# Attention scores of four heads on own 32 rows, masked in PSUM, with one exp per group

## The chip, the cores and the metric

The kernel runs on one core of a Trainium2 chip. The time is the device time of one execution in microseconds; the number given is the median of several runs. The profile is one traced execution; its span, from the first to the last instruction, is a little shorter than the time of a run.

Names of the engines in the profile: PE is TensorE (matrix products), PEld its weight loads, DVE is VectorE, ACT is ScalarE, POOL is GpSimd and SP is SyncE, which here only issues transfers.

## The reference, cut to what matters

Two independent parts stand side by side in the output.

Part A is a long convolution: a 4-tap shift of `k`, times `v`, convolved over 2048 positions with `ssm_k` for each of 640 channels (an FFT in the reference), plus a skip term, times `q`.

Part B is attention with 32 heads of 20 dimensions, in four segments of 512 tokens that are attended causally, and a memory of the earlier segments:

```python
for s in range(N):                                   # N = 4, L = 512, Dh = 20
    logits = einsum('bhqd,bhkd->bhqk', qs, ks) * scale + mask    # mask: -1e9 above the diagonal
    p = softmax(logits)
    a_dot = einsum('bhqk,bhkd->bhqd', p, vs)
    pq = phi(qs)                                     # phi(t) = t + 1 or exp(t)
    a_mem = (pq @ M) / (pq @ z + 1e-6)
    o = g * a_mem + (1 - g) * a_dot
    M, z = M + phi(ks).T @ vs, z + sum(phi(ks))
return o @ wo
```

The change touches the line of the logits, its mask and the exp in the softmax, and how all the work is ordered.

## The kernel before, in words

Everything is recorded first and emitted in another order. `Recorder` stands in for the engines: each call becomes an `Op` with its dependences, and all products into one PSUM bank until another engine reads it form one `Op`. `plan` (line 236) then lists the work: it prices each operation by a small model (`price`), walks forward and backward with priorities from the tables `BIAS` and `HOLD`, keeps the best of seven orders, and gives banks to operations. `emit` (line 430) issues the calls in that order, so nearly every row of the profile carries the line number 435. Each engine executes its own instructions in the order emitted.

Part A is cut into five slices of 128 channels. For each slice: the shift as 16 products of 128 columns per bank (`kshift`, tiles `kr`, `skd`), a forward transform of two signals (`fwd`, `Wf` with `vt` and `kT`), butterflies and a pointwise product on VectorE (tiles `F`, `Xh`, `Kh`, `pr`, `S`), and an inverse transform (`inverse`, `Wi` with `S`). `kT` is reordered by a copy on VectorE before it is transposed.

Part B is cut into eight units `u` of one segment and half of the heads (16). For each unit: `proj` (line 688) makes K, Q and V for four blocks of 128 tokens; ScalarE copies K and Q to `KQ`, with each head's 20 values in a slot of 32, and two transposing transfers write `KT` and `QT`, where one head occupies 32 partitions and four heads fill 128. `bound` (line 710) computes for each query an upper bound of its logits, negated, and writes it by four small transfers into row 20 of each head in `QT`; row 20 of K holds ones, so the product subtracts the bound and the exp cannot overflow. I call it the bound row. Four groups `g` of four heads follow.

In `attn` (line 764) a score product contracts all 128 partitions, so one head's keys have to stand alone: `spread` (line 757) copies K from `KT` into `KZ`, where each head has its own zero-filled copy with only its 21 rows set. For a pair of heads and each of three specifications of key blocks (block 0: 512 columns; blocks 1 and 3 together: 384 + 128; block 2: 256), a product fills a bank `st` and an exp on ScalarE writes it to `ET`, transposed scores with keys on partitions. Then VectorE multiplies the diagonal blocks of `ET` by the triangle `cmask`, in two instructions per group of heads, and products of 21 columns (`o<-Va,ET`) sum over the keys; one more product per 128 queries reads the memory (`Mbd`, `PqT`). VectorE divides and writes `o_s`, which is transposed to `oT` and multiplied by `wo` once both halves of a segment are there.

PSUM has eight banks of 512 fp32 columns. They are dealt to four kinds of work: three for scores, two for part A, two for projections and one for `o`.

```python
BANKS = {"st": 3, "a": 2, "b": 2, "o": 1}      # line 836
```

Of the kernel before, what the change touches and what calls it, by code (L numbers as in the profile page):

```python
# [42 lines left out]
def small_consts():  # L43
    p = np.arange(128)
    d = p % 32
    hl = p // 32
    sel = np.zeros((128, 4, 16), np.float32)
    for g in range(4):
        ok = d < DH
        sel[p[ok], g, 4 * hl[ok] + g] = -1.0  # L50
    maskbd = np.zeros((128, 4, VW), np.float32)
    epsrow = np.zeros((128, 4), np.float32)
    for hh in range(4):
        rows = (hl == hh) & (d < DH)
        maskbd[rows, hh, 0:DH + 1] = 1.0
        epsrow[32 * hh + DH + 1, hh] = EPS
    kk = np.arange(128)[:, None]; qq = np.arange(128)[None, :]
    cmask = (kk <= qq).astype(np.float32)
    return sel.astype(BF16_NP), maskbd.astype(BF16_NP), epsrow, cmask.astype(BF16_NP)
# [21 lines left out]
class Op:  # L81
    __slots__ = ("eng", "calls", "key", "bank", "new", "dur", "lat", "dma", "pred", "succ", "tail", "idx", "late")


class Bank:
    def __init__(self, kind, home):
        self.kind, self.home, self.left, self.last, self.ops, self.seq = kind, home, 0, None, [], 0
# [6 lines left out]
class Recorder:  # L94


    def __init__(self, tc):
        self.tc, self.real = tc, tc.nc
        self.nc = ProxyNC(self)
        self.ops, self.key = [], ("const",)  # L100
        self.live, self.masks = {}, {}
        self.slots, self.home, self.turn, self.rows = {}, {}, {}, {}
# [5 lines left out]
    def bank(self, kind):  # L108
# [3 lines left out]
        b = self.home[t[:].tensor.name] = Bank(kind, t[:].tensor.name)  # L112
        b.row = kind if kind in ("st", "o") else self.key[0] if kind == "b" and self.key[0] == "P" else None
        if b.row:
            b.seq = self.rows.get(b.row, 0)
            self.rows[b.row] = b.seq + 1
# [18 lines left out]
    def add(self, eng, method, args, kw):  # L135
# [12 lines left out]
        if op is None:  # L148
            op = Op()
            op.eng, op.calls, op.key, op.bank, op.dma, op.idx = e, [], self.key, bank, None, len(self.ops)  # L150
            op.new = bank is not None and bank.last is None
            op.pred, op.succ, op.dur, op.lat = {}, [], 0.0, 0.0
            self.ops.append(op)
            if bank is not None:
                bank.left += 1
                bank.ops.append(op)
# [3 lines left out]
        self.price(op, method, outs[0], ins)  # L160
# [18 lines left out]
    def price(self, op, method, out, ins):  # L179
        n = int(np.prod(list(out.shape)[1:]))  # L180
        two = lambda a: mybir.dt.size(a.dtype) == 2
        if method == "matmul":
            op.dur += max(n / 2.4 + 2.5, 27.0)
            op.lat = 260.0
        elif method in ("dma_start", "dma_start_transpose"):
            src = ins[0]
            size = int(np.prod(list(out.shape))) * mybir.dt.size(out.dtype)
            if method == "dma_start_transpose":
                packets, per = size / 256, 23.5
                dram = src.space == bass.MemoryType.DRAM  # L190
                op.dur = 650.0 + 560.0 * size / 131072 + (600.0 if dram else 0.0)
            else:
                run = min(self.run(out), self.run(src))
                packets, per = size / run, max(23.0, 13 + 0.042 * run)
                op.dur = 640.0 if op.eng != "ACT" else 650.0
            op.dma = packets * per / 16
            op.lat = 1200.0
        elif op.eng == "ACT":
            op.dur, op.lat = n / 1.152 + 33, 210.0
        elif op.eng == "DVE":  # L200
            fast = all(two(a) and a.space != bass.MemoryType.PSUM and int(a.ap[-1][0]) == 1 for a in [out] + ins)
            if method == "tensor_tensor":
                op.dur = n / (1.92 if fast else 0.96) + 60
            elif method == "tensor_reduce":
                op.dur = int(np.prod(list(ins[0].shape)[1:])) / 0.96 + 60
            elif method == "reciprocal":
                op.dur = 67 + 6.1 * n
            else:
                op.dur = n / (3.84 if fast else 1.2) + 60
            op.lat = 150.0  # L210
        else:
            op.dur, op.lat = 100 + n / 1.2, 200.0

    @staticmethod
    def run(ap):
        r = mybir.dt.size(ap.dtype)
        need = 1
        pat = list(ap.ap)[1:] if ap.space != bass.MemoryType.DRAM else list(ap.ap)
        for st, n in reversed(pat):
            if st != need:  # L220
                break
            r *= n
            need *= n
        return r

    def finish(self):
        for o in self.ops:
            o.dur, o.lat = int(round(o.dur)), int(round(o.lat))
            o.dma = None if o.dma is None else int(round(o.dma))
            if o.new and o.bank.kind == "a":  # L230
                for q in o.bank.ops[1:]:
                    for p in q.pred.values():
                        if p.bank is not o.bank:
                            o.pred[p.idx] = p

    def plan(self, bias, hold, passes, slack):

        ops = self.ops
        for o in ops:
            o.succ = []  # L240
        for o in ops:
            for p in o.pred.values():
                p.succ.append(o)
        for o in ops:
            o.late = list(o.pred.values())
        for o in ops:
            if o.new:
                for b in o.bank.ops[1:]:
                    for q in o.succ:
                        if q.bank is not o.bank and b not in q.late:  # L250
                            q.late.append(b)
        for o in reversed(ops):
            o.tail = max([q.tail for q in o.succ], default=0) + o.dur + (o.dma or 0) + o.lat
        load = [o.dma is not None and o.dma > 0 and o.key[0] in ("load", "A", "P", "const") and len(o.pred) <= 1 for o in ops]
        best = None
        prio = [-(o.tail + bias.get(o.key, 0)) for o in ops]
        held = [hold.get(o.key, 0) if o.dma is not None else 0 for o in ops]
        for n in range(passes + 1):
            total = self.forward(prio, held)
            if best is None or total < best[0]:  # L260
                best = (total, self.order, self.slot, self.start, self.done)
            if n == passes:
                break
            back, end = self.backward([-(self.start[o.idx] + o.dur) for o in ops])
            lead = [end - b for b in back]
            prio = [s - (bias.get(o.key, 0) >> 3) for o, s in zip(ops, lead)]
            held = [max(0, s - slack - hold.get(o.key, 0)) if l else 0 for o, s, l in zip(ops, lead, load)]
        _, self.order, self.slot, self.start, self.done = best
        return best[0]

    @staticmethod
    def lag(o):
        return o.lat if o.dma is None else max(1150 - o.dur, -50) + o.dma + 450

    def backward(self, prio):
        ops = self.ops
        need = [0] * len(ops)
        for o in ops:
            for p in o.late:
                need[p.idx] += 1  # L280
        ready = [0] * len(ops)
        free = {e: 0 for e in ("PE", "DVE", "ACT", "POOL", "SP")}
        pending, avail = {e: [] for e in free}, {e: [] for e in free}
        empty = {k: [0] * len(v) for k, v in self.slots.items()}
        row = {k: n - 1 for k, n in self.rows.items()}
        left, held = {}, set()
        times = [0]
        for o in ops:
            if need[o.idx] == 0:
                ready[o.idx] = self.lag(o)  # L290
                heapq.heappush(pending[o.eng], (ready[o.idx], o.idx))
                times.append(ready[o.idx])
        heapq.heapify(times)
        back, count = [0] * len(ops), 0
        while times:
            t = heapq.heappop(times)
            while times and times[0] <= t:
                heapq.heappop(times)
            for e in free:
                pe, av = pending[e], avail[e]  # L300
                while pe and pe[0][0] <= t:
                    i = heapq.heappop(pe)[1]
                    heapq.heappush(av, (prio[i], -i))
                if free[e] > t:
                    continue
                put_back, o = [], None
                while av:
                    x = heapq.heappop(av)
# [654 lines left out]
```

## Time and profile before

| what | value |
|---|---|
| time, median of 3 runs | 358.62 us (356.18 to 363.19) |
| profiled span | 353.7 us |
| busy share of PE, DVE, ACT, POOL | 86%, 86%, 79%, 23% |
| mean granted clock of TensorE | 0.970 |
| chain that ended last | PE 33%, DVE 28%, issue 14%, DMA 8%, ACT 6% |
| exps of scores (`ET<-st`) | 384 instructions, 185.2 us busy |
| score products (`st<-QT,KZ`) | 508 recorded, 105.1 us busy |
| masks (`ET<-ET,cmask`) | 64 instructions, 43.0 us busy |
| spreads (`KZ<-KT`) | 64 issues on GpSimd, 40.0 us busy |

Three engines are busy for four fifths of the span or more, and the chain of waits passes from one to another all the time, so no single row is the bound. Busy time is the union of the instructions' durations. On TensorE and ScalarE instructions overlap, so the mean duration of a row times its count is more than its busy time, and both are more than the time that the engine needs for it. The page's 40 slices show a head of about five slices with little ScalarE work, a long full stretch, and a short tail. It helps to ask for busy time by stretch and to read single rates off the timeline, where an unbroken run of equal instructions gives the time of one.

### The profile page before, as it was taken

The numbers are of one execution on the slowest core, as the hardware profiler recorded it, in microseconds if no ns is written. First come the engines' busy times: TensorE is split into PE (matmuls) and PEld (weight loads), VectorE is DVE, ScalarE is ACT, GpSimd is POOL, SyncE is SP. The second block draws the span as 40 slices with busy tenths as digits, with TensorE's granted clock in tenths as the row PEclk, the third lists the DMA queues.
The fourth block names the chain that finished last, engine by engine and source line by source line (L and its number), as shares of the span: only waits on it lengthen the run. The fifth ranks groups of instructions, "written<-read, shape, count | busy, mean of one in ns | idle before, by whom it ended". The sixth has DMA issues, their size and how long they took to land.

```text
span 353.7 us, 9016 instructions
## 1 busy us (share of the span) xinstructions
PE 302.4 (86%) x3462; PEld 217.8 (62%) x3466; DVE 305.7 (86%) x539; ACT 278.0 (79%) x633; POOL 80.5 (23%) x127
## 2 busy tenths in 40 slices
PE   0179699899997699799999999999989998888584
PEld 0157477567785477577766776777766675555363
DVE  2016999999999999899999999999998998999960
ACT  1046648999979989889989999989986998899502
POOL 9402410214112110312024005230060040312023
PEclk9999999999999899899999999999998999999869
DMA  9976766969557335705598358537430564302043
GB/s 262 212 141 165 159 141 98 256 117 199 112 114 186 73 62 113 134 17 74 150 130 202 74 126 142 117 68 105 100 92 26 91 105 70 92 30 69 0 101 110
DMA packets 110267, 40.97 MB, mean 116 GB/s; under 512 B 102624, under 2 KB 107264, under 8 KB 109968
## 3 DMA queue, kind: packets, MB, share of 16 engines
q1 hardware_dynamic: 100768, 29.50, 43.7%
q0 software_dynamic: 5088, 8.09, 8.9%
q10 hardware_dynamic: 4368, 2.81, 2.8%
q8 instruction: 27, 0.44, 0.5%
q14 instruction: 16, 0.13, 0.1%
HBM read 13.36 MB, written 5.24 MB: 53 GB/s over the span
## 4 chain that ended last, share of the span: by engine, by line
PE 33%; DVE 28%; issue 14%; DMA 8%; ACT 6%; SPq 6%; POOL 3%; POOLq 0%; ACTq 0%; DVEq 0%
PE b L435 13%; PE a L435 9%; PE st L435 7%; DVE S L435 7%; SPq L435 6%; PE o L435 4%; DVE ET L435 4%; DMA KT<-KQ 3%; DVE Xh L435 3%; ACT ET L435 3%; DVE kam L435 3%; DMA kr<-in_A_k_dram 2%; POOL out_dram L435 2%; DMA oT<-o_s 1%; DVE o L435 1%
## 5 line engine op out<-in xcount | busy, mean ns | idle before, releaser
L435 ACT ACTIVATE ET<-st 128x512 bf16<-128x512 f32 (+1 forms) x384 | 185.2, 575 | 11.6 <-PE st L435 10.5
L435 PE MATMUL st<-QT,KZ 128*128 128x384 bf16 (+2 forms) x508 | 105.1, 301 | 6.3 <-ACT ET L435 3.9
L435 PE MATMUL b<-wqkv,xT 128*128 128x320 bf16 x480 | 79.3, 303 | 18.8 <-DMA xT<-in_B_x_dram 16.0
L435 PEld LDWEIGHTS <-xT 128*128 128x128 bf16 x480 | 45.8, 99 | 37.6 <-DMA xT<-in_B_x_dram 16.0
L435 POOL DMA_DIRECT2D KZ<-KT x64 | 40.0, 629 | 123.0 <-PE st L435 91.1
L435 PEld LDWEIGHTS <-KZ 128*128 128x128 bf16 x512 | 45.6, 98 | 28.0 <-issue 12.2
L435 PEld LDWEIGHTS <-ET 128*128 128x128 bf16 x1280 | 41.8, 96 | 24.1 <-DVE ET L435 11.5
L435 PE MATMUL o<-Va,ET 128*128 128x21 bf16 x1280 | 44.2, 173 | 12.0 <-DVE ET L435 5.9
L435 ACT CAST F<-a 128x512 bf16<-128x512 f32 x80 | 48.4, 624 | 5.5 <-PE a L435 5.0
L435 ACT CAST KQ<-b 128x320 bf16<-128x320 f32 x64 | 30.0, 472 | 19.4 <-PE b L435 17.4
L435 DVE TENSOR_TENSOR ET<-ET,cmask 128x1024 bf16<-128x1024 bf16 x64 | 43.0, 682 | 0.4 <-ACT ET L435 0.4
L435 PEld LDWEIGHTS <-Wf 128*128 128x128 bf16 x320 | 30.3, 99 | 15.8 <-issue 8.8
L435 DVE TENSOR_TENSOR S<-S 128x2048 bf16<-128x2048 bf16 (+1 forms) x40 | 37.2, 950 | 0.2
L435 POOL DMA_DIRECT2D out_dram<-outa x20 | 15.4, 769 | 71.5 <-DVE outa L435 52.7
L435 PE MATMUL b<-wo,oT 128*128 128x320 bf16 x160 | 28.0, 314 | 0.6 <-DMA oT<-o_s 0.6
L435 PE MATMUL a<-kT,Wf 128*128 128x256 bf16 x160 | 24.3, 274 | 2.9 <-DVE outa L435 1.9
L435 ACT CAST outb<-b 128x320 bf16<-128x320 f32 x32 | 14.9, 480 | 14.1 <-PE b L435 14.1
L435 DVE TENSOR_TENSOR o<-o,rr 128x320 bf16<-128x320 f32 x48 | 23.6, 491 | 1.6
L435 PE MATMUL a<-vt,Wf 128*128 128x256 bf16 x160 | 23.3, 280 | 1.4 <-ACT F L435 0.7
L435 PE MATMUL a<-S,Wi 128*128 128x256 bf16 x160 | 22.2, 286 | 1.5 <-DVE S L435 1.5
L435 DVE TENSOR_TENSOR S<-Xh,Kh 128x4096 bf16<-128x4096 bf16 x10 | 22.8, 2284 | 0.1
L435 PE MATMUL a<-skd,kr 128*128 128x128 bf16 x320 | 22.0, 224 | 0.4 <-DMA kr<-in_A_k_dram 0.2
(61 smaller groups left out, 385.0 us busy)
## 6 DMA issues: line engine op xcount, KB each, us to landing
KZ<-KT POOLq DMA_DIRECT2D x64, 42.0 KB, 2.9
kT<-in_A_ssm_k_dram SPq DMA_DIRECT2D x5, 512.0 KB
qd<-in_A_q_dram SPq DMA_DIRECT2D x20, 128.0 KB
out_dram<-outa POOLq DMA_DIRECT2D x20, 128.0 KB, 2.8
out_dram<-outb POOLq DMA_DIRECT2D x16, 160.0 KB, 2.1
vt<-in_A_v_dram SPq DMA_DIRECT2D x16, 128.0 KB
Wf<-c_wf ACTq DMA_DIRECT2D x1, 1024.0 KB
Wi<-c_wi SPq DMA_DIRECT2D x1, 1024.0 KB
```

The source lines that it names most:

```text
L435: f(*[fix(a) for a in args], **{k: fix(v) for k, v in kw.items()})
```

## The change

The change has four parts.

1. **Scores on own rows.** K and Q of a unit go into one tile `KQT`, by one transposing transfer instead of two. The score product of head `hl` reads only that head's rows, `32*hl` to `32*hl + 20`, of K and of Q. `KZ` and its spreads are gone. The four heads of a group stand on four separate sets of 32 rows of the array and write four separate banks.
2. **One exp.** The four banks are one tile `st` of 2048 columns, and one exp reads all four heads: three exps per group of heads (2048, 2048 and 1024 columns) instead of twelve.
3. **Masks in PSUM.** Before the scores a product of the identity with `later` (0 on and below the diagonal, -1e9 for keys later than the query) is written to each diagonal block, and the score product adds to it. VectorE's masks are gone.
4. **One pool and a stored order.** The other four banks are one pool `w` for all other work. There is no planner: the order of the operations is stored as a compressed list, and each group takes the bank that has been free longest. Some operations change place: the `kT` copies go from VectorE to ScalarE; most plain loads and the bound rows go from the queues of SP and ACT to GpSimd's; `Wf` is loaded in four pieces.

The purpose is to relieve VectorE of the masks, ScalarE of the fixed cost of many small exps, GpSimd and the transfer engines of the spreads, and to let four products with a short contraction share the array.

```diff
-        QT, PqT, Va = self.QT[half], self.PqT[half], self.Va[half]
+        KQT, PqT, Va = self.KQT[half], self.PqT[half], self.Va[half]
+        QT = KQT[:, 4:8, :]
...
-        def spread(gg):
-            def f():
-                for hl in range(4):
-                    rows = slice(32 * hl, 32 * hl + DH + 1)
-                    nc.gpsimd.dma_start(out=self.KZ[gg][rows, :, hl, :], in_=self.KTs[u][rows, 2 * gg:2 * gg + 2, :])
-            return f
...
-                for hp in range(2):
-                    for spec in (((0, 0),), ((1, 0), (3, 384)), ((2, 0),)):
-                        sts = [self.bank("st") for j in range(2)]
-                        width = 0
-                        for j in range(2):
-                            hl = 2 * hp + j
-                            for (kc, c0) in spec:
-                                n = L - 128 * kc
-                                nc.tensor.matmul(sts[j][:, c0:c0 + n], lhsT=KZ[:, g % 2, hl, 128 * kc:128 * kc + 128], rhs=QT[:, g, 128 * kc:L], start=True, stop=True)
...
-                        for j in range(2):
-                            nc.scalar.activation(out=ET[:, 2 * hp + j, e0:e0 + width], in_=sts[j][:, 0:width], func=ACTF.Exp, scale=SCALE)
-                for (c0, step) in ((0, 512), (896, 128)):
-                    blk = ...
-                    V.tensor_tensor(out=blk, in0=blk, in1=self.cmask[:, None, None, :].to_broadcast([128, 4, 2, 128]), op=ALU.mult)
+                for spec in (((0, 0),), ((1, 0), (3, 384)), ((2, 0),)):
+                    st = self.bank("st")[:].rearrange("p (h q) -> p h q", h=4)
+                    nd = len(spec)
+                    for hl in range(4):
+                        blk = st[:, hl, 0:128] if nd == 1 else st[:, hl, :].rearrange("p (b q) -> p b q", q=128)[:, 0:4:3, :]
+                        later = self.later[:] if nd == 1 else self.later[:, None, :].to_broadcast([128, 2, 128])
+                        nc.tensor.matmul(blk, lhsT=self.ident[:], rhs=later, start=True, stop=False, skip_group_check=True)
+                    for (kc, c0) in spec:
+                        n = L - 128 * kc
+                        for hl in range(4):
+                            rows = slice(32 * hl, 32 * hl + DH + 1)
+                            nc.tensor.matmul(st[:, hl, c0:c0 + n], lhsT=KQT[rows, g, 128 * kc:128 * kc + 128], rhs=KQT[rows, 4 + g, 128 * kc:L],
+                                             start=False, stop=True, skip_group_check=True)
+                    width = max(c0 + L - 128 * kc for (kc, c0) in spec)
+                    e0 = ET_OFF[spec[0][0]]
+                    nc.scalar.activation(out=ET[:, :, e0:e0 + width], in_=st[:, :, 0:width], func=ACTF.Exp, scale=SCALE)
...
-                nc.sync.dma_start_transpose(out=self.KTs[u][:, :, tok], in_=KQ[:, 0, :, :])
-                nc.sync.dma_start_transpose(out=QT[:, :, tok], in_=KQ[:, 1, :, :])
+                nc.sync.dma_start_transpose(out=KQT[:, :, tok], in_=KQ[:])
...
-                nc.sync.dma_start(out=QT[r:r + 1, :, :], in_=bT[4 * hl:4 * hl + 4, :])
+                nc.gpsimd.dma_start(out=KQT[r:r + 1, 4:8, :], in_=bT[4 * hl:4 * hl + 4, :])
...
-            nc.vector.tensor_copy(out=skp[:], in_=sk.rearrange("d (b p c) -> d c b p", b=4, c=4))
+            nc.scalar.copy(out=skp[:], in_=sk.rearrange("d (b p c) -> d c b p", b=4, c=4))
...
-BANKS = {"st": 3, "a": 2, "b": 2, "o": 1}
+BANKS = {"st": (1, 2048), "w": (4, 512)}
...
-    rec.finish()
-    rec.plan(BIAS, HOLD, PASSES, SLACK)
+    order = np.frombuffer(zlib.decompress(base64.b85decode(ORDER)), np.uint16).tolist() if ORDER else range(len(rec.ops))
     with tc.manual_schedule():
-        rec.emit()
+        rec.emit(order)
```

## The prediction

> **What bounds the kernel now.** I read the page's first two parts, then busy time by stage, then the groups by shape, then the timeline where single costs can be read off. The page alone does not name a bound:
>
> ```profile
> PE 302.4 (86%) x3462; PEld 217.8 (62%) x3466; DVE 305.7 (86%) x539; ACT 278.0 (79%) x633; POOL 80.5 (23%) x127
> ```
>
> The stretches do. I cut the span at the first and last exp of scores (53.4 and 333 us; columns as in the header):
>
> ```profile
> core 0: us, PE busy (x) PEld busy (x) DVE busy (x) ACT busy (x) POOL busy (x), PEclk, DMA share, GB/s
> 0.00:53.40 53.40, 31.57 (x292) 22.99 (x293) 27.22 (x46) 20.64 (x44) 19.47 (x30) 1.00 0.80 179
> 53.40:333.00 279.60, 257.16 (x3057) 185.26 (x3058) 269.48 (x478) 254.00 (x582) 55.86 (x89) 0.98 0.53 106
> 333.00:354.00 21.00, 13.71 (x116) 9.57 (x116) 9.05 (x17) 3.41 (x8) 5.21 (x8) 0.74 0.35 89
> ```
>
> In the 279.6 us of the score stage VectorE is busy 269.5 us, 96%. That stage is VectorE-bound, and TensorE (92%) and ScalarE (91%) are close behind; the other 74 us are a head that waits for loads and a tail. Two groups of the score stage, all from the table by shape:
>
> ```profile
> L435 ACT ACTIVATE ET<-st 128x512 bf16<-128x512 f32 x256 | 146.0, 647 | 9.9 <-PE st L435 9.3
> L435 ACT ACTIVATE ET<-st 128x256 bf16<-128x256 f32 x128 | 48.8, 431 | 1.7 <-PE st L435 1.2
> L435 DVE TENSOR_TENSOR ET<-ET,cmask 128x1024 bf16<-128x1024 bf16 x64 | 43.0, 682 | 0.4 <-ACT ET L435 0.4
> L435 DVE COPY kT<-kT 128x2048 bf16<-128x2048 bf16 x5 | 7.3, 1467 | 4.2 <-DMA kT<-in_A_ssm_k_dram 4.2
> ```
>
> Busy time of PE and ACT includes overlapped latency, so I take rates from unbroken runs in the timeline:
>
> ```profile
> 26.68 0.23 PE L435 MATMUL a<-Drow,cmask 1*128 1x128 bf16 x1
> 26.84 0.39 PE L435 MATMUL a<-kT,Wf 128*128 128x256 bf16 x2
> 27.16 0.22 PE L435 MATMUL a<-Drow,cmask 1*128 1x128 bf16 x1
> 27.32 2.61 PE L435 MATMUL a<-kT,Wf 128*128 128x256 bf16 x16
> 30.05 1.95 PE L435 MATMUL a<-skd,kr 128*128 128x128 bf16 x32
> ...
> 61.14 2.08 ACT L435 ACTIVATE ET<-st 128x512 bf16<-128x512 f32 x4
> 63.06 0.64 ACT L435 CAST F<-a 128x512 bf16<-128x512 f32 x1
> ```
>
> 32 products of 128 columns take 1.95 us, less a 0.22 us latency of the last: 0.056 us each. In the same way 256 columns take 0.109, 320 columns 0.136, 384 about 0.162, 512 0.216 and the 21-column products 0.026 us. Four exps of 512 columns take 1.92 us to the next instruction: 0.478 each, that is 0.833 ns per column and 0.05 us. One alone lasts 0.61 us (0.38 for 256), so its end, which a waiting TensorE sees, comes after 0.833 ns per column and 0.18 us. In the waits between the two engines ACT starts 0.04 us after the product's end, and PE 0.05 us after the exp's end.
>
> **What the Trainium skill says.** "TensorE: Matmul & The Clock Gate", Part 3 (Packing small matmuls): products on different groups of 32 rows run concurrently in the array; four with K=32 and N=512 measured 3.07 times faster. No product of the kernel before is packed, so the trace cannot confirm it. "TensorEngine Tiling (Array Packing)", Key Properties: changing the tiling mode drains TensorE. The trace agrees and prices it: the one-row Drow product uses a 32-row tile; two 256-column products before it would stream in 0.22 us, but it starts 0.32 us after them, and the next full product starts 0.16 us after it instead of 0.056. Each switch costs 0.10 us. The same page, PSUM Pressure: different row tiles must write different banks, which is why the four heads get four banks. "ScalarE: Activation LUTs", What ACT_TABLE_LOAD costs: 0.833 ns per element, a fixed part of 186 ns for an instruction with immediate operands, and about 93 ns overlap of neighbours. The trace has 0.833, 180, and 130 ns overlap.
>
> **The change part by part.**
>
> *VectorE.* The 64 masks (43.0 us) go, and the five kT copies (7.3 us) move to ACT. In the score stage that is 41.6 + 3.9 us, so VectorE falls from 269.5 to 224 us there. It stops being the bound.
>
> *ScalarE.* Of 384 exps 96 remain: 64 of 2048 columns, 32 of 1024. Throughput before 256 x 0.478 + 128 x 0.265 = 156 us; after 64 x 1.76 + 32 x 0.90 = 141 us. The five copies add 5 x 1.8 = 9 us (the 2048-column PqT row lasts 1.91). Net about -6 us: ScalarE hardly gets lighter. Its other work between the first and last exp sums to 90 us by the order, 230 us in all.
>
> *TensorE.* Score products streamed 128 x (0.216 + 0.162 + 0.109 + 0.056) = 69.5 us. After, per score group of four heads: identity products 4 x 0.056 = 0.22 us (0.44 for the group with two diagonals), one mode switch in (0.10), then the packed scores. Three 0.026 us issue steps and the stream make 0.216 + 0.08 = 0.29 us for 512 columns (the skill's 3.07 would give 0.28), 0.34 for 384 + 128, 0.19 for 256. So 0.62, 0.88 and 0.51 us, 2.0 us per four heads, 64 us in total, plus 96 switches back, 9.6 us. TensorE's stream is thus the same as before, about 74 for 70 us: packing pays for the masks. Unpacked, the scores would take 0.86, 0.87 and 0.44 us and the total becomes 107 + 9.6 us.
>
> *The new wait.* One four-bank score buffer instead of three: group n+1's identity products wait on TensorE's in-order queue until exp n has ended, and everything behind them waits too. Conversely exp n+1 waits on ACT's queue for the group, with evacuations behind it. Round trip seen by TensorE: exp end (1.89 or 1.03 us), plus 0.25 us for both hand-overs and the product's latency: 2.13 and 1.28 us. The stored order puts other products in this gap. Summing the products between neighbouring score groups of the new PE order with the rates above, switch back included: 2.20 us on average behind a long exp, 1.39 behind a short one. Each gap costs the larger of filling and round trip: 2.33 x 64 + 1.46 x 31 = 194.3 us. Add the score groups, 63.3 us: 257.6 us. In 26 gaps ACT's own evacuations are longer than that, +6 us: 263.5 us for the stage if nothing else interrupts.
>
> *Losses on top.* A clock of 0.98 in this stage, as before, is 2% of 247 us of TensorE stream: 5 us. Before, the stage lost 10 us over its bound; with four banks for all other groups instead of five, and two engines now locked together, I take 7 us (0 to 25). Stage: 275 us.
>
> *Head and tail.* Before the first score group stand 228 products, 24.0 us of stream, instead of 288; the bound row goes through GpSimd's queue, KZ's spread (64 transfers) no longer stands between KT and the scores, and K and Q come in one transpose. Loads still hold the first product (16.0 us in the trace). I take the first exp at 46 us (43 to 52) instead of 53.4. At the end the last mask stood behind other VectorE work (exp over at 332.7, product at 339.5), which now vanishes; the transposes, output projection and store remain: 17 us (15 to 21) instead of 21.
>
> *Hidden anyway.* Transfers moved from SP to GpSimd: its queue sheds 64 spreads (40.0 us at 0.63 each) and takes 77 issues (32 bound rows, 20 loads of q, 16 of v, 4 of ssm_k, five of weights), some 48 us of a 23% busy engine. Behind a load that waits for its buffer stand, in order, bound rows and stores; the scores of a later unit wait for the rows, which the order issues a unit ahead, so I charge nothing beyond the losses above. Wf in four pieces: inside the head.
>
> Sum: 46 + 275 + 17 = 338 us of span. The median was 4.9 us above the profiled span (358.6 against 353.7), so the time is 343 us.
>
> **The rivals.** (a) *The packed products do not overlap*, or overlap little. For it: no trace here shows packing, and identity products at full height alternate with them. Against: the skill's measurement, and separate banks. The same sum gives 302 us; with 12 us of losses, 46 + 314 + 17 + 4.9 = 382 us, slower. (b) *The single buffer locks PE and ACT together*: each late transfer, VectorE result or missing bank now delays both, with no spare score bank to absorb it. For it: ACT is above 90% and three banks absorbed such jitter. Against: the order's fillings match the round trip. With 27 us of losses the stage takes 290 to 295, the time 355 to 361, no change. (c) *Losses nearly vanish*, since VectorE at 224 us releases banks early: stage 264, head 43, tail 16, time 328.
>
> **How the numbers follow.** Forecast 0.60, (c) 0.12, (b) 0.16, (a) 0.12. The prediction is the likeliest case, 343 us. The range runs from (c)'s value, 328, to past (b), 366: it leaves out (a) and a fast corner, under 2 in 10. Below 351.4 us are the forecast and (c): 0.72; within 2% (b): 0.15; above: 0.13.
>
> **What would show it.** VectorE about 255 us busy with no mask row; exp rows near 1.89 and 1.03 us; packed 512-column score products starting about 0.03 us apart rather than 0.22, which decides (a); score stage near 275 us, with the waits "PE st from ACT ET" and "ACT ET from PE st" short and frequent; first exp near 46 us. I am wrong if the four products of a group stand one after the other, if waits on w banks or on ACT exceed some 30 us on PE, or if the bound row's path through GpSimd delays the first scores.

## The result, and the profile after

| what | before | after |
|---|---|---|
| time, median of 5 runs each | 362.04 us (356.18 to 365.87) | 337.92 us (334.0 to 343.83) |
| ratio, 95% interval | | 0.940 (0.929 to 0.951) |
| ratio when measured again (`after_again`) | | 0.933 (0.926 to 0.940) |

The change takes 6 to 7% off, 22 to 24 us. The first profiled execution of the changed kernel was a longer one than its median, so the lines below are from the second, of 336.64 us; likewise the profile of the old order without masks, of an execution of 1581.65 us, isn't read, and that of the added VectorE load is of an execution 3 us over the mean of those in its ratio.

The page, its first lines and the chain that ended last:

```profile
span 334.8 us, 9219 instructions
...
PE 291.8 (87%) x3850; PEld 208.6 (62%) x3850; DVE 263.3 (79%) x470; ACT 268.0 (80%) x350; POOL 82.1 (25%) x139
...
PE 47%; DVE 14%; DMA 13%; ACT 12%; issue 8%; POOL 2%; SPq 2%; ACTq 0%; POOLq 0%; DVEq 0%
```

VectorE lost 42 us of busy time and its share of the chain fell from 28% to 14%; TensorE's share rose from 33% to 47%. Now the three stretches, cut at the first and the last exp as before (columns: us; busy us of PE, PEld, DVE, ACT, POOL; clock; DMA share; GB/s):

```profile
0.00:48.80 48.80, 28.70 (x241) 19.99 (x242) 17.20 (x38) 21.63 (x43) 11.37 (x28) 0.97 0.83 172
48.80:320.80 272.00, 255.17 (x3528) 182.83 (x3529) 243.09 (x427) 243.14 (x299) 66.92 (x105) 0.96 0.54 104
320.80:335.00 14.20, 7.97 (x85) 5.78 (x82) 3.05 (x8) 3.21 (x8) 3.84 (x7) 0.97 0.47 118
```

The head lost 4.6 us, the score stage 7.6 (279.6 to 272.0), the tail 6.8: 19 us of the 22 to 24, since the profile of the kernel before is of an execution shorter than its median. This split compares two single executions. The head varies most: in three traces of the old order the first exp comes at 53.0, 53.4 and 59.4 us, in six of the new one, those without the memset of the last experiment, at 48.4 to 51.3. The score stage also took in work that the kernel before did outside it: VectorE's busy time in the head fell from 27 to 17 us. In the stage VectorE is now 89% busy instead of 96%, ScalarE 89%, TensorE 94%.

The groups by shape, and two lines of the waits (us, times, longest):

```profile
L191 ACT ACTIVATE ET<-st 128x2048 bf16<-128x2048 f32 x64 | 121.5, 1898 | 11.0 <-PE st L191 9.9
...
L191 ACT ACTIVATE ET<-st 128x1024 bf16<-128x1024 f32 x32 | 33.5, 1047 | 7.9 <-PE st L191 7.8
...
L191 PE MATMUL st<-later,ident 128*128 128x128 bf16 x256 | 25.4, 223 | 3.3 <-ACT ET L191 2.8
...
L191 PE MATMUL st<-KQT 21*128 21x512 bf16 x128 | 12.7, 388 | 0.0
```

```profile
ACT ET L191 <- PE st L191: 17.7, 26, 2.4
...
PE st L191 <- ACT ET L191: 7.6, 11, 1.7
```

The same two waits in the kernel before:

```profile
ACT ET L435 <- PE st L435: 10.5, 22, 1.7
...
PE st L435 <- ACT ET L435: 3.9, 12, 0.7
```

One group of four heads on TensorE's timeline (start, us), with the products behind it:

```profile
77.80 0.39 PE L191 MATMUL st<-later,ident 128*128 128x128 bf16 x4
78.12 0.39 PE L191 MATMUL st<-KQT 21*128 21x512 bf16 x4
78.45 0.85 PE L191 MATMUL w<-wqkv,xT 128*128 128x320 bf16 x5
```

96 exps of 1.90 and 1.05 us stand where 384 stood, and no row of masks is left on VectorE. The row `st<-KQT` of 512 columns shows the packing at once: 128 products, each 0.388 us long, were busy for 12.7 us together, so four run side by side. On the timeline, four of them take the array for 0.33 us (78.12 to 78.45). With the single score buffer, ScalarE waited in 26 of the 96 hand-overs and TensorE in 11, 25 us in all; with three banks it was 14 us. What a second buffer would save was not tried.

### The profile page after: what moved, and what is told of

Its sections match the earlier page's. It is cut to its first block, busy times and chain, and to the rows that moved or that the text cites. A ratio compares the mean times of both kernels' runs of the same rounds, so it can differ in the third digit from the quotient of the medians.

```text
span 342.1 us, 9219 instructions
## 1 busy us (share of the span) xinstructions
PE 292.9 (86%) x3850; PEld 209.6 (61%) x3850; DVE 263.1 (77%) x470; ACT 268.6 (79%) x350; POOL 82.3 (24%) x139
## 4 chain that ended last, share of the span: by engine, by line
PE 43%; DVE 21%; DMA 14%; ACT 9%; issue 9%; POOL 2%; SPq 0%; POOLq 0%; DVEq 0%; ACTq 0%
PE w L191 34%; PE st L191 9%; DMA KQT<-KQ 8%; DVE S L191 6%; ACT ET L191 5%; DMA xT<-in_B_x_dram 4%; DVE Kh L191 2%; DVE pr L191 2%; ACT F L191 2%; DVE kam L191 2%; DMA vt<-in_A_v_dram 2%; DVE o L191 1%; POOL out_dram L191 1%; DVE outa L191 1%; DVE Xh L191 1%
## 5 line engine op out<-in xcount | busy, mean ns | idle before, releaser
L191 ACT ACTIVATE ET<-st 128x2048 bf16<-128x2048 f32 (+1 forms) x96 | 154.7, 1612 | 20.5 <-PE st L191 19.4
L191 PE MATMUL w<-wqkv,xT 128*128 128x320 bf16 x480 | 79.5, 311 | 18.6 <-DMA xT<-in_B_x_dram 16.4
L191 PEld LDWEIGHTS <-xT 128*128 128x128 bf16 x480 | 45.4, 101 | 42.4 <-DMA xT<-in_B_x_dram 16.4
L191 PE MATMUL st<-later,ident 128*128 128x128 bf16 (+1 forms) x384 | 45.5, 242 | 8.3 <-ACT ET L191 7.9
L191 ACT CAST F<-w 128x512 bf16<-128x512 f32 x80 | 44.8, 606 | 1.4 <-PE w L191 1.3
L191 PEld LDWEIGHTS <-ident 128*128 128x128 bf16 x384 | 31.8, 100 | 19.0 <-issue 13.7
L191 PE MATMUL w<-Va,ET 128*128 128x21 bf16 x1280 | 43.4, 173 | 0.0
L191 ACT CAST KQ<-w 128x320 bf16<-128x320 f32 x64 | 26.5, 449 | 13.6 <-DMA KQT<-KQ 8.9
L191 PE MATMUL st<-KQT 21*128 21x512 bf16 (+3 forms) x512 | 35.6, 309 | 0.4 <-DMA KQT<-bT 0.4
L191 PE MATMUL w<-wo,oT 128*128 128x320 bf16 x160 | 25.6, 299 | 2.4 <-DVE o L191 1.3
L191 PE MATMUL w<-vt,Wf 128*128 128x256 bf16 x160 | 23.6, 277 | 1.3 <-DVE xm L191 0.6
```

What stands on the lines that cost most here:

```text
L191: f(*[fix(a) for a in args], **{k: fix(v) for k, v in kw.items()})
```

## The experiments

Every ratio is to the kernel before on the same chip, with its 95% interval. All runs of the changed kernel are to be held against 0.933. They undo one part and keep the stored order, which stands for all parts together; with an order of its own each of them might lose less.

### The changed kernel again

> The changed kernel itself, for a second profile. Its first profile has first exp at 49.5 us, 279.3 us from first to last exp (279.6 in the kernel before), and a tail of 14 us, with one stop of TensorE and ScalarE of 7 us near 96-103 us, when KQT transposes wait among 16 other loads. Theory 1 (VectorE was the bound of the score stage and its relief pays): an ordinary run has a stage of 268-274 us, first exp 46-49, span 332-337, ratio about 0.94; the stop near 100 us is shorter or gone. Theory 3 (the stage is not shorter, only head and tail are): stage within 3 us of 279.6, span 340.

Ratio 0.933 (0.926 to 0.940), profile as above: the stage is 272.0 us, 7.6 us shorter where theory 3 allowed 3, so theory 3 falls by this one execution, though head and tail together (11.4 us) gave more than the stage. The stop near 96 us is short here: ScalarE waited 2.39 us for a KQT transpose at 86 us.

### Masks back on VectorE

```diff
-                        nc.tensor.matmul(blk, lhsT=self.ident[:], rhs=later, start=True, ...)
+                for (c0, step) in ((0, 512), (896, 128)):
+                    blk = ET[...]
+                    V.tensor_tensor(out=blk, in0=blk, in1=self.later[...], op=ALU.mult)
```

Here `later` holds ones and zeros, and the score products start their banks themselves.

> In the changed kernel the masks go back to VectorE: the identity products are left out and the two multiplications of ET per group of heads stand where the exp that they need ends; everything else, with its order, stays. VectorE gets 64 x 0.68 = 43 us back, TensorE loses 32 x 0.88 = 28 us. Theory 1: VectorE is the bound again, 244 + 42 = 286 us busy in the stage, which with 2-4% idle gives 292-298 us, ratio 0.99-1.01 (355-362 us). Theory 2 (packing is what pays, VectorE had slack left): TensorE is lighter, so no slower than the changed kernel, ratio 0.90-0.95.

Ratio 1.084 (1.072 to 1.096): 54 us more than the changed kernel, beyond every expectation. Its stage, and its waits:

```profile
48.40:375.70 327.30, 251.93 (x3146) 166.31 (x3147) 279.57 (x488) 245.68 (x299) 66.29 (x104) 0.88 0.41 85
```

```profile
DVE ET L192 <- ACT ET L192: 37.3, 31, 3.7
...
PE w L192 <- DVE o L192: 27.0, 18, 3.0
...
ACT ET L192 <- PE st L192: 26.2, 20, 3.3
```

VectorE is only 280 of 327 us busy, so its load alone doesn't set this stage. A mask must wait for its exp; VectorE's queue stood 37.3 us in 31 such waits, TensorE waited for the results queued behind (27.0 us), and ScalarE for TensorE's scores (26.2 us). The masks stand right behind their exps, where the stored order had no place for them. The clock of this stage is lower too, 0.88 instead of 0.96, and no run separates it from the waits.

### The load of the masks without their wait

```diff
+                    if spec[0][0] > 0:
+                        blk = self.load[...]          # a tile that nothing else uses
+                        V.tensor_tensor(out=blk, in0=blk, in1=self.later[...], op=ALU.mult)
```

> The changed kernel with 64 more VectorE instructions of the masks' form (128x1024, 0.68 us each) on a tile that nothing else uses: 43 us of load, 42 in the score stage, no wait for an exp and nobody waiting for them; the identity products stay. If the VectorE load as such was the price: 243 + 42 = 285 us busy in the stage, which takes 288-298 us, ratio 0.98-1.01. If it was the wait between exp, mask and product that cost the 55 us with masks on VectorE: 0-8 us more, ratio 0.935-0.955.

Ratio 0.987 (0.983 to 0.991), 19 us above 0.933, or above 0.934 for the kernel that shares this one's memset (the hold below). The stage:

```profile
44.30:343.80 299.50, 259.67 (x3527) 184.31 (x3526) 278.26 (x491) 245.35 (x299) 67.58 (x105) 0.95 0.51 94
```

VectorE is again over 90% busy (278 of 299.5), and the load as such has a price, as the first of the two expectations says. So about 19 of the 54 us come with the load alone. The other 35 come with the waits and with the lower clock of the run before (0.88; here 0.95).

### No masks at all in the changed kernel

```diff
-                        nc.tensor.matmul(blk, lhsT=self.ident[:], rhs=later, start=True, stop=False, ...)
```

> The changed kernel without any mask: the identity products are left out and nothing takes their place, so the attention is not causal. TensorE loses 28 us of stream. If TensorE together with the hand-over to ScalarE paces the stage (my sum): 15-28 us shorter, ratio 0.86-0.90. If VectorE (244 us busy in 279) or ScalarE (about 235 us of throughput) still paces it: 0-8 us shorter, ratio 0.92-0.94.

Ratio 0.937 (0.931 to 0.943): no gain. The stage takes 270.6 instead of 272.0 us, with TensorE 232.6 busy instead of 255.2:

```profile
51.30:321.90 270.60, 232.62 (x3146) 160.77 (x3147) 242.34 (x426) 241.46 (x299) 66.50 (x104) 0.94 0.55 103
```

The chain that ended last:

```profile
PE 22%; DVE 21%; DMA 20%; ACT 20%; issue 10%; POOL 3%; SPq 1%; POOLq 0%; DVEq 0%; ACTq 0%
```

So the masks cost the changed kernel nothing: TensorE takes them in time that it would otherwise wait. TensorE alone isn't its bound, although it has 47% of the chain: without the masks its share falls to 22%, those of VectorE, ScalarE and the transfers rise, and the time stays. This contradicts the sum of the prediction, by which the stage had to become 15 to 28 us shorter.

### Full-height score products

```diff
-    lhsT=KQT[rows, g, 128 * kc:128 * kc + 128], rhs=KQT[rows, 4 + g, 128 * kc:L]
+    lhsT=KQT[:, g, 128 * kc:128 * kc + 128], rhs=KQT[:, 4 + g, 128 * kc:L]
```

> The score products of the changed kernel read all 128 rows of K and Q instead of 32 each, so each computes the sum over four heads and four of them can't stand side by side; no change of tiling mode any more. Per four heads TensorE streams 4 x (0.216 + 0.162 + 0.056 + 0.109) = 2.17 us of scores instead of 0.85, and saves 0.6 us of mode changes: +0.7 us, +23 us in all, and the round trip grows as long. Theory 2 (packing pays, TensorE is near its limit): +18 to +30 us, ratio 0.99-1.03. Theory 1 alone (TensorE has slack once VectorE is relieved): +0 to +8 us, ratio 0.94-0.965.

Ratio 0.989 (0.980 to 0.998): 20 us more, within theory 2's 18 to 30. The stage and the chain:

```profile
49.50:338.20 288.70, 276.53 (x3500) 215.79 (x3527) 243.90 (x424) 246.04 (x299) 66.92 (x105) 1.00 0.49 97
```

```profile
PE 71%; ACT 10%; DMA 8%; issue 6%; POOL 2%; SPq 1%; DVE 1%; POOLq 0%; ACTq 0%; DVEq 0%
```

TensorE is 96% busy and 71% of the chain. Packing is needed: without it, nearly all that the change gains is gone. Together with the last run: TensorE has no gain left in it, and no room either.

### Four exps instead of one

```diff
-    nc.scalar.activation(out=ET[:, :, e0:e0 + width], in_=st[:, :, 0:width], func=ACTF.Exp, scale=SCALE)
+    for hl in range(4):
+        nc.scalar.activation(out=ET[:, hl, e0:e0 + width], in_=st[:, hl, 0:width], func=ACTF.Exp, scale=SCALE)
```

> The changed kernel with the one exp over four banks cut into four over one bank each, placed one after the other. Each costs ScalarE 0.05 us more: 288 x 0.05 = 14.7 us, and the hand-over back to TensorE comes 0.15 us later. If ScalarE together with the hand-over paces the stage: 10-20 us more, ratio 0.96-0.99. If ScalarE has slack: 0-5 us more, ratio 0.935-0.95.

Ratio 0.955 (0.947 to 0.963), from two executions: 8 us more, just under the first band and over the second. About half of 14.7 us of ScalarE time comes through.

### The kernel before without masks, planned anew

```diff
-                for (c0, step) in ((0, 512), (896, 128)):
-                    blk = ...
-                    V.tensor_tensor(out=blk, in0=blk, in1=self.cmask[...], op=ALU.mult)
```

> The kernel before without its two masks per group of heads: the attention is not causal, and the planner orders the rest anew. Theory 1 (VectorE, 269 of 280 us busy, bounds the score stage): VectorE falls to about 228 us there and the stage to what ScalarE and TensorE allow, 12-25 us less, ratio 0.93-0.965. Theory 3 (the score stage is not what the change shortens): 0-5 us less, from the tail alone, ratio 0.985-1.0.

Ratio 1.004 (1.000 to 1.007). By the numbers expected theory 1 falls. But the first exp now comes at 61.3 us instead of 53.4:

```profile
0.00:61.30 61.30, 35.39 (x308) 25.81 (x309) 33.10 (x49) 20.45 (x43) 19.37 (x30) 0.97 0.71 166
61.30:340.90 279.60, 256.78 (x3082) 188.46 (x3089) 238.62 (x423) 253.14 (x583) 58.56 (x93) 0.98 0.53 105
```

The planner chose another order, with more work ahead of the first score (308 products instead of 292; TensorE's wait for xT is the same, 16.1 us and 16.0), and VectorE is only 85% busy in a stage as long as before. Two things changed at once, so the next three kernels kept the order.

### The kernel before in its own order: no masks, shorter exps, both

The plan is made with the masks; the edits are at the issue. The first leaves out the masks, the second shortens the exps:

```diff
             for eng, method, args, kw in o.calls:
+                if eng == "vector" and "in1" in kw and is_ap(kw["in1"]) and kw["in1"].tensor.name == self.mask:
+                    continue
...
+                if eng == "scalar" and kw.get("out") is not None and kw["out"].tensor.name in self.ets:
+                    n = int(kw["out"].ap[-1][1])
+                    cut = n * 456 // 512
+                    kw = dict(kw, out=kw["out"][:, 0:cut], in_=kw["in_"][:, 0:cut])
```

With the shorter exps, VectorE also sets the two buffers of `ET` to zero at the start, 2.19 us each.

> The kernel before in exactly its own order, planned with the masks, but the 64 mask instructions are not issued (attention not causal): 43 us of VectorE work gone, nothing else moved on any engine. Theory 1 (VectorE bounds the score stage): 15-25 us less there and up to 5 in the tail, ratio 0.92-0.955. Theory 4 (three engines in balance, in fixed orders that wait on each other, so that relief of one alone buys little): 2-8 us less, ratio 0.975-0.995. If the new order was what spoiled the run without masks and with a new plan (no gain), this run gains; if not, it is at 1.0 again.

> The kernel before in its own order, but each exp covers 456 of 512 or 228 of 256 columns, the rest of ET is zero from the start: 256 x 0.0467 + 128 x 0.0233 = 14.9 us of ScalarE throughput gone, as much as the one exp over four banks saves. Theory 1: ScalarE isn't the bound, 0-4 us less, ratio 0.99-1.0. Theory 4: 2-8 us less, 0.975-0.995. If ScalarE is the bound: 11-15 us less, 0.957-0.97.

> Both of these: no mask instructions and the shorter exps, in the order of the kernel before. Theory 1: as without masks alone, or 3-5 us less than that (0.91-0.95), since ScalarE becomes the next bound. Theory 4: clearly more than the sum of the two single gains, 18-28 us less, 0.92-0.95, while each alone stays at 0.975 or above.

| in the order of before | ratio | us |
|---|---|---|
| no masks | 0.970 (0.964 to 0.976) | -11 |
| shorter exps | 0.996 (0.992 to 1.000) | -2 |
| both | 0.950 (0.941 to 0.960) | -18 |

The stages with shorter exps alone, then with both:

```profile
59.40:338.60 279.20, 256.34 (x3057) 184.62 (x3058) 269.03 (x478) 242.96 (x582) 56.32 (x89) 0.98 0.54 106
```

```profile
53.00:318.60 265.60, 251.42 (x3070) 184.72 (x3073) 235.74 (x415) 240.52 (x582) 56.03 (x89) 0.99 0.56 111
318.60:337.80 19.20, 12.22 (x102) 8.70 (x101) 7.83 (x15) 3.42 (x8) 5.23 (x8) 0.79 0.42 97
```

With ScalarE 11 us lighter and VectorE still 96% busy, the stage stays at 279 us. It starts at 59.4 us because in this execution TensorE waited for xT until 21.9 us instead of 16.0; that moves it, but not its length. With VectorE lighter as well the stage falls to 265.6. So of these two engines VectorE was the first bound, as theory 1 has it, but of 43 us taken from it only 11 come through: less than theory 1's 15 to 25 and more than theory 4's 2 to 8. Relief of TensorE alone was not tried in this order. Once the masks are gone, ScalarE's relief is worth 7 us where it was worth 2. The sum of the single gains is 3.5%, both together 5.0%, from two executions; the difference is barely outside the intervals.

### The kernel before with scores on own rows

```diff
-    lhsT=KZ[:, g % 2, hl, 128 * kc:128 * kc + 128], rhs=QT[:, g, 128 * kc:L]
+    lhsT=KT[rows, g, 128 * kc:128 * kc + 128], rhs=QT[rows, g, 128 * kc:L]
```

> The kernel before with its score products on the 32 rows of each head: no KZ, no spreads, two buffers of KT, four of outb, everything else as it was (two banks for two heads, four exps of 512 per two heads, masks on VectorE); the planner orders anew, and two neighbouring products of different heads can stand side by side. TensorE is relieved by up to half of 70 us of score stream, less some 0.1 us per change of tiling mode (up to 2 x 192, so 10-38 us net gain at most). Theory 1 (VectorE bounds the stage): 0-6 us less, ratio 0.98-1.0. Theory 2 (TensorE's stream bounds it): 12-25 us less, ratio 0.93-0.965.

Ratio 1.050 (1.043 to 1.057), slower, which neither theory expected. The stage:

```profile
61.60:355.80 294.20, 280.47 (x3024) 161.90 (x3023) 264.49 (x468) 253.68 (x576) 20.85 (x33) 0.90 0.43 89
```

TensorE is busy for 280 us instead of 257, but its clock is 0.90 instead of 0.98, and 257 x 0.98 / 0.90 is 280: the clock alone would account for the longer busy time, and no relief by packing shows. By the starts in the trace, only 116 of 512 score products begin within 10 ns of the score product ahead of them, and the order goes over from other products to scores 166 times; in the changed kernel it is 383 of 512 and 96. It looks as if own rows pay only where the order puts the heads next to each other in different banks, but this is not shown. The run doesn't decide between the theories, because the order is new as well and the clock lower, and what lowers the clock stays open.

### Loads held back at the start

```diff
+        nc.gpsimd.memset(self.load[:], 0.0)      # 4.4 us, ahead of GpSimd's loads
```

> The changed kernel with one GpSimd memset of 4.4 us on an unused tile ahead of its queue of loads, nothing else. In the run with the added VectorE load, which had this memset too, xT landed 10.8 us after its issue instead of 14.9, since the three weight loads of 400 KB from GpSimd's queue started 4.3 us later, and the first exp came at 44.3 us instead of 48.8. If the head's gain stays: 3-5 us less than the changed kernel, ratio 0.918-0.926. If something later waits for the delayed weights or takes it back: ratio 0.93-0.94.

Ratio 0.934 (0.928 to 0.940): no gain. The chain of the changed kernel, then of this one, near its start and near 80 us:

```profile
2.01 14.93 DMA xT<-in_B_x_dram
...
78.61 7.71 DMA KQT<-KQ
```

```profile
2.02 11.07 DMA xT<-in_B_x_dram
...
43.03 1.88 ACT ET L192
...
81.88 14.27 DMA KQT<-KQ
96.14 0.02 issue
96.16 0.02 ACTq L192
96.18 0.04 issue
96.22 0.43 ACT KQ L192
96.66 0.04 issue
96.70 1.87 PE w L192 x8
```

The head's gain is there: xT lands 3.9 us sooner, and the first exp comes at 43.0 instead of 48.8 us. In this execution it is given back 50 us later. A KQT transpose takes 14.27 us instead of 7.71; the copy to KQ waits for it, TensorE waits for the copy, and both stand for over 7 us. Busy time and DMA share by tens of microseconds (changed kernel ahead):

```profile
80.00:90.00 10.00, 7.58 (x98) 5.02 (x97) 8.64 (x14) 7.61 (x12) 3.66 (x5) 0.91 1.17 238
90.00:100.00 10.00, 10.00 (x117) 6.83 (x115) 8.84 (x16) 9.17 (x17) 0.00 (x0) 0.91 0.75 137
```

```profile
80.00:90.00 10.00, 9.45 (x115) 6.38 (x114) 9.73 (x17) 8.67 (x14) 2.83 (x4) 1.00 1.11 162
90.00:100.00 10.00, 3.30 (x24) 1.87 (x24) 5.11 (x9) 3.30 (x6) 0.00 (x0) 0.70 0.66 65
```

The DMA engines are full just then (share 1.1), with the loads of `Wi` (1 MB), `wo` (800 KB), `qd`, `vt` and `kT` that the change put on GpSimd's queue. That these loads delay the transposes is read from this overlap; moving them was not tried. Nor does the overlap explain the length: in the changed kernel the share is 1.2 in the same stretch and the transpose takes 7.71 us, and in the changed kernel's longer execution, of 343.83 us, one takes 14.3 us without any hold. So the hold is not what makes a transpose slow; only that the time gained nothing is shown.

## Why the prediction was right

343 us was forecast, 337.9 measured, inside the range. The direction holds, and so does the main step, that packing pays for the masks. That the sum comes so close is in part luck: the head was 2.8 us longer than forecast, the stage 3.0 and the tail 2.8 shorter, and the stage came out although one engine's load in it and the term that was to pace it were wrong. Point by point:

- **VectorE bounds the score stage; the masks' removal ends that.** Right against ScalarE: in the order of before, relieving ScalarE alone left the stage at 279 us, relieving VectorE saved 11 us of the whole time. The size of its relief was off. I subtracted whole rows (50.3 us), but rows of VectorE overlap too, and the union fell by 42.4; and 10 us of its head work moved into the stage. It is 243 us busy there, not 224, so it still stands beside ScalarE (243) and TensorE (255).
- **Packing pays for the masks.** Right, and without this step most of the gain does not come: unpacked, 20 of 24 us are lost. The size was too cautious. I took issue steps of 0.026 us, held up by the 3.07 times of "TensorE: Matmul & The Clock Gate"; the starts in the trace lie 3 to 4 ns apart. The same page of the Trainium skill has that too, about 4 ns per further product (Measured speedup vs the span model), and the trace agrees: it was the figure to take. The time from the first identity product to the first product after the scores is 0.65, 0.86 and 0.54 us for the three groups (medians), 2.05 us per four heads, where I had 2.31 with the switch back: 66 instead of 74 us. The switch itself was right: 0.15 us from the last identity product to the first score (0.056 + 0.10), and 0.317 us from the last of four 512-column scores to the next full product (0.216 + 0.10).
- **One exp.** 1.90 and 1.05 us where I had 1.89 and 1.03. Cutting it into four costs 8 of the 14.7 us of ScalarE time.
- **The single score buffer.** I summed the larger of filling and round trip over all gaps, 263.5 us, and added 12 of losses, 275. The stage took 272. But this sum is not what sets the stage: by it the run without identity products had to be 15 to 28 us shorter there, and it was 1.4 us shorter. VectorE and ScalarE are each busy for 243 us of it, so either may hold it where TensorE does not, and a clock of 0.94 instead of 0.96 may have taken some of what that run spared TensorE. The lock of rival (b) did not come: the waits between the two engines rose from 14 to 25 us together.
- **Head.** 46 us forecast, 48.8 measured. I left the first product at 16.0 us; here it waited for xT until 17.0 us, which is 1 us of the 2.8, and the rest isn't traced. In the six traces of the new order without the hold it waited until 16.0 to 17.1 us, in the two with the memset until 12.8 and 13.1: the weight loads that moved to GpSimd's queue do delay xT. The hold also shows that ending this gains nothing in the whole time.
- **Transfers to GpSimd, charged at nothing.** Wrong in that place: I named what is queued behind a waiting load on GpSimd, but not that its big loads share the DMA engines with the KQT transposes on SP's queue, which hold the KQ buffer. ScalarE's longest wait for such a transpose was 2.4 and 7.6 us in two executions of the changed kernel. How much of it the loads cause is open.
- **Tail.** 17 us forecast, 14.2 measured, but not mainly for the reason that I gave. Without masks (and with shorter exps) the old order still has a tail of 19.2 us of 21.0. Of the rest, 4 us are products: the changed kernel has 8.0 us of them left after the last exp, the old order without masks 12.2. Fewer products (85 for 102) and a clock of 0.97 instead of 0.79 go together there.
- **From span to time.** I added 4.9 us, the difference of the earlier median and the profiled span. That profile was simply of a shorter execution: one execution of the changed kernel has 336.64 us for a span of 334.8. This 3.1 us and the 3.2 us of span (338 against 334.8) are the whole miss for that execution.

The rivals: (a) did not come; its price, which I put at 382 us with all switches left in, is 356.5 us when the switches go too. For (b), a stage of 290 to 295 us gives 358 to 363 us by the other terms, not the 355 to 361 that I wrote. (c) had 328 us with a stage of 264, where 272 was measured; what keeps it from there is not shown.

How much each part gives can't be added up, since the parts share one balance: masks off VectorE and 15 us less of exps give 18 us even in the old order, where nothing is paid for the masks; the change, with packing to pay for them, gives 22 to 24. What the stored order, the pool of four banks and the moved loads give by themselves wasn't separated.

## What to carry to other kernels

Here three engines were each over 90% busy in one stage. Relieving the most loaded one gained only down to the next, 11 us for 43. Putting load back on one cost between four and nine tenths of it: 19 us for 43 on VectorE, 8 for 14.7 on ScalarE, 20 for the 23 expected on TensorE. So move work to an engine together with something that frees it there: the masks were free on TensorE in a kernel whose scores were packed in the same change; with the same masks and the scores unpacked, 20 of the 24 us were lost. And undo one part with the order of the others kept; a new plan alone moved the first exp by 8 us and hid an 11-us gain.

## What the hardware showed that I had not expected

- Packed scores alternate with full-height products 96 times, at a price of two mode changes of 0.10 us each: four products that would stream 0.864 us one after the other (4 x 0.216) let the next full product start 0.327 us after the first of them, with the change back included. With the change before them it is 0.42 us, about half of 0.864.
- The granted clock in the stage was 1.00 with full-height scores (TensorE 96% busy), 0.96 in the changed kernel (94%), 0.94 without identity products (86%), 0.90 with own rows in the old kernel (95%) and 0.88 with masks on VectorE (77%). Part 1 of "TensorE: Matmul & The Clock Gate" in the Trainium skill says that activity releases the throttle. These traces agree only in part: in the stop of the hold TensorE is 3.3 of 10 us busy and the clock 0.70, but 95% busy goes with 0.90 in one run and 96% with 1.00 in another. Whether 32-row products count for less activity stays open.
- One and the same transposing transfer, 128 rows of 1024 values, can take 3 us or 14: with the hold, KQT transposes landed in 3.0 us at the least, 3.7 in the median, 14.3 at the most, the last while the DMA engines were full.
